# A Fourier transform feeding a gated layer: VectorE's PSUM reads in a row, GpSimd's sums and folds behind a wait, two buffers for folded chunks

## The chip, the cores and the metric

The kernel runs on one core of one Trainium2 chip. The metric is the device time of one execution in microseconds (us). A core has five engines with instruction queues of their own: TensorE (PE in the profile; PEld is its weight load), VectorE (DVE), ScalarE (ACT), GpSimd (POOL) and SyncE (SP, which here only issues DMAs). They wait for each other by semaphores. SBUF is the on-chip memory, PSUM the accumulators that TensorE writes.

## The reference, cut to what matters

```python
x                       # 8 x 3008 x 256, float32
X = fft(fft(x, axis=1), axis=2).real      # rows become 24064 tokens of 256
h = X @ w_in            # w_in 256 x 2048
g = h * cos(h)
out = g @ w_out         # w_out 2048 x 256
```

## The kernel before, in words

The Fourier transform over the 256 columns is folded into the weights `w_in` once, at the start. The transform over the 3008 rows is done for each of 8 batches in two halves by matmuls with constant matrices. *First half*: the batch is loaded (`load_x`, in two parts) and cut into 8 chunks. `fold` (L240) adds and subtracts mirrored columns of a chunk into the buffer `xf`, on GpSimd for all batches but the first, with a small column copy on ScalarE (L247). `first_half` multiplies it (pz, L282 and L285), ScalarE copies the result (zs), and `store_z` sends it to DRAM. *Second half*: `load_z` brings it back, `second_half` (pb, L327) makes six groups of it, `pq`, with a row `nb` for each group that goes out and back by DMA. A group holds 256 tokens (225 in group 0, whose steps are the "short" ones), and each is worked on together with its mirror image in the batch: side sg = 0 and side sg = 1.

The layer then runs in *steps*. A step is one group and one of 8 pairs of blocks of the 2048 hidden columns, so there are 8 steps in a group, 48 in a batch, 384 in all. The main loop (L741) writes out by hand the order in which step t of each part is issued, as a software pipeline: `cur` is step t, `prev` t-1, `old` t-2, `done` t-3. For one step s the parts are:

- `seed` (ScalarE, L453): puts the norm's part of h into a PSUM bank H, one step ahead. Three banks H rotate.
- mm1 (TensorE, L483), first half with WC, then second half with WS, both added into H. Between them `act_e` (ScalarE, L494) copies the first half's result times two into `ew`.
- h (VectorE, L499, `dve_h`): `ew` minus H, the mirror side. It reads H in PSUM.
- two roundings (ScalarE, L514) of H and of h into r.
- frac0 and frac1 (VectorE, L518, `dve_frac`): r minus H and r minus h. The first reads H in PSUM, the second reads only SBUF.
- the sin (ScalarE, L524) over both sides, after frac1.
- g0 and g1 (VectorE, L528, `dve_g`): (H - 0.25) r and (h - 0.25) r. The first reads PSUM, the second only SBUF.
- s0, s1, s2 (VectorE, L539, L546, L548, `dve_s` with k = 0, 1, 2): sums of r into S, which let seven products stand for eight. All read only SBUF.
- mm2 (TensorE, L572): seven matmuls m0 to m6, in the trace two instructions each, four before mm1's second half of a later step and three behind it. m6, alone in the group M<-S,w, is the one that reads what s2 wrote.

VectorE's order in one pass of the loop is g0(old), g1(old), frac0(prev), s0(old), frac1(prev), s1(old), h(cur), s2(old). TensorE's is mm1(cur) first half, m0 to m3 of done, mm1(cur) second half, m4 to m6 of done.

When a group's 8 steps are through, ScalarE takes the seven sums out of PSUM (mr, L593), GpSimd adds them up with six instructions (L611 to L621, into `cb`), and `store_out` transposes `cb` on VectorE (L664), once for each side, and issues the output DMAs on SyncE. The six sums are issued in a row; only their inputs hold them up. The transposes come two and three steps after `take_m`'s first part. For the last group `combine_last` does all this on VectorE, TensorE and ScalarE.

The next batch's transform is spread over the steps of the current one by `transform`, a table from a step's number in the batch to calls: x loaded at steps 3 and 14, chunk folds at 6, 9, 14, 17 and so on (both halves of a fold in the same step), their first halves 2 or 4 steps later, z stored one step after that, z loaded at 39, and the six second halves at 42 to 47.

Of the kernel before, what the change touches and what calls it, by code (L numbers as in the profile page):

```python
# [121 lines left out]
def kernel(  # L122
# [102 lines left out]
    nc.gpsimd.memset(xf[0:XR, 512:1024:128], 0.0)  # L225

    bank = {"fft": 1, "M": 4, "H": 3}

# [2 lines left out]


    def folded(b, c):
        return xf if b else xf0[c % 2]

    def fold(b, c, e):
        lo = IP * (c % 4)
        xv = xs[c // 4].rearrange("r (i d) -> r i d", d=ND)[0:XR, lo : lo + IP]
        fv = folded(b, c).rearrange("r (e i d) -> r e i d", e=2, d=128)[0:XR]
        (nc.gpsimd if b else nc.vector).tensor_tensor(  # L240
            out=fv[:, e, :, 1:128],
            in0=xv[:, :, 1:128],
            in1=xv[:, :, 255:128:-1],
            op=ALU.subtract if e else ALU.add,
        )
        if e == 0:
            (nc.scalar.copy if b else nc.gpsimd.tensor_copy)(  # L247
                out=fv[:, 0, :, 0], in_=xv[:, :, 0]
            )

    def middle(b, p):
        xm = xs[p].rearrange("r (i d) -> r i d", d=ND)[0:XR, :, 128]
# [67 lines left out]
    def second_half(b, g):  # L320

        T = _width(g)
        z2 = z2s[b]
        pb = psum("pb")
        for q in range(4):
            jj = 4 * g + q
            nc.tensor.matmul(  # L327
                pb[:, 128 * q : 128 * q + 128],
                lhsT=z2[:, jj * 128 : jj * 128 + 128],
                rhs=BJ[:, jj * 128 : jj * 128 + 128],  # L330
                start=True,
                stop=True,
            )
# [12 lines left out]
        if b == 0 and g == 0:  # L346
            return
        nd = dpool.tile([1, 256], FP, tag="nd", bufs=4, name="nd")
        nc.sync.dma_start(out=nd[:, 0:T], in_=pq[0:1, T : 2 * T])
        nc.sync.dma_start(out=nb[:, 0:T], in_=nd[0:1, 0:T].to_broadcast([128, T]))  # L350


    def spread_norm():
# [3 lines left out]
        nc.tensor.matmul(pn[:, 0:T], lhsT=ones, rhs=pq[0:1, T : 2 * T], start=True, stop=True)  # L357
        nc.scalar.copy(out=nb[:, 0:T], in_=pn[:, 0:T])

    def transform(b):  # L360
        todo = {}

        def at(o, *call):
            todo.setdefault(o, []).append(call)
# [167 lines left out]
    def dve_s(s, k):  # L532
        T = s.T
        gv = s.r[:, 0 : 4 * T].rearrange("p (q t) -> p q t", q=4)
        if k == 0:
            s.S = spool.tile([128, 1024], FP, tag="S", bufs=2, name="S")
        sv = s.S[:, 0 : 4 * T].rearrange("p (q t) -> p q t", q=4)
        if k == 0:
            nc.vector.tensor_tensor(  # L539
                out=sv[:, 0:2],  # L540
                in0=gv[:, 2:3].to_broadcast([128, 2, T]),
                in1=gv[:, 0:4:3],
                op=ALU.subtract,
            )
        elif k == 1:
            nc.vector.tensor_tensor(out=sv[:, 2], in0=sv[:, 1], in1=gv[:, 0], op=ALU.subtract)  # L546
        else:
            nc.vector.tensor_tensor(out=sv[:, 3], in0=gv[:, 1], in1=sv[:, 2], op=ALU.add)  # L548

    def mm2(s, part):  # L550
        T = s.T
# [47 lines left out]
    def combine_m(s):  # L599
        T = s.T  # L600
        key = (s.b, s.grp)
        acc.pop(key)
        mv = mrs.pop(key).rearrange("p (m t) -> p m t", m=7)[:, :, 0:T]
        cb = spool.tile([128, 7 * 256], FP, tag="cb", bufs=1, name="cb")
        cf = cb.rearrange("p (m t) -> p m t", m=7)
        cv = [cf[:, m, 256 - T : 256] if m in (2, 3) else cf[:, m, 0:T] for m in range(7)]
        if T < 256:
            nc.gpsimd.memset(cf[:, 0:2, T:256], 0.0)
            nc.gpsimd.memset(cf[:, 2:4, 0 : 256 - T], 0.0)
        tt = nc.gpsimd.tensor_tensor  # L610
        tt(out=cv[0], in0=mv[:, 0], in1=mv[:, 1], op=ALU.add)  # L611
        tt(out=cv[4], in0=mv[:, 0], in1=mv[:, 5], op=ALU.subtract)
        tt(
            out=cf[:, 5:7, 0:T],
            in0=cf[:, 4:5, 0:T].to_broadcast([128, 2, T]),
            in1=mv[:, 3:5],
            op=ALU.add,
        )
        tt(out=cv[1], in0=cv[6], in1=mv[:, 6], op=ALU.add)
        tt(out=cv[2], in0=cv[5], in1=mv[:, 2], op=ALU.add)  # L620
        tt(out=cv[3], in0=cv[5], in1=mv[:, 4], op=ALU.add)  # L621
        outs[key] = cb

    def combine_last(s):
        key = (s.b, s.grp)
# [111 lines left out]
    def step(t, last=None):  # L737
        s = steps[t] if 0 <= t < n else None
        return s if s is not None and (last is None or s.fp == 7) else None

    for t in range(n + LAG + 1):  # L741
        cur, prev, old, done = step(t), step(t - 1), step(t - 2), step(t - LAG)
        if cur:
            if t % per == 0:
                todo = transform(cur.b + 1) if cur.b + 1 < NB else {}
            mm1(cur, 0)
            act_e(cur)
            if t == 0:
# [44 lines left out]
        for call in todo.pop(t % per, ()):  # L793
            call[0](*call[1:])


# [28 lines left out]
```

## Time and profile before

| | |
|---|---|
| median of 3 runs | 1974.6 us (1972.9 to 1975.87) |
| the profiled execution's own time | 1975.47 us |
| its span, first to last instruction | 1973.7 us |
| mean granted TensorE clock | 0.994 |
| busy: TensorE, VectorE, ScalarE, GpSimd | 1946.2, 1858.0, 1504.2, 467.7 us |

The span is taken in the execution that was profiled, so terms from the trace are set against that execution's own time. In rows of groups the columns are line, engine, operation, output<-input and count, then busy time in us, mean ns of one instruction, then the idle time of the engine just ahead of them and what ended it. In rows of the timeline they are the start in us, the duration in us, the engine, line, operation, output<-input and count; in brackets the idle time before and what released it. TensorE's ends are modelled, so its pace is better read from starts.

### The profile page before, as it was taken

To read this page: it belongs to the slowest core of one execution; us is meant where nothing else is said; L and a number is where in the kernel's file an instruction comes from. 1 tells how busy PE (TensorE), PEld (TensorE's weight loads), DVE (VectorE), ACT (ScalarE), POOL (GpSimd) and SP (SyncE) were. 2 spreads that over 40 slices of the span, in tenths; PEclk is the share of its full clock that TensorE was granted. 3 is DMA by queue.
4 is the path that set the end of the run, shared out by engine and by line. 5 is a ranking of instruction groups with operands and counts; after the bars stand their busy time and mean duration, and the time that the engine had idled before them with its cause. 6 is when DMAs were issued, how large, how long until landed. Compare 5 with 4: busy or idle time off the path is not lost.

```text
span 1973.7 us, 28641 instructions
## 1 busy us (share of the span) xinstructions
PE 1946.2 (99%) x9216; PEld 1686.8 (85%) x9216; DVE 1858.0 (94%) x3217; ACT 1504.2 (76%) x2762; POOL 467.7 (24%) x431
## 2 busy tenths in 40 slices
PE   7999999999999999999999999999999999999998
PEld 3888899888988889888898888988889888898887
DVE  4999989999899998999989999999999999899998
ACT  2877777777777778777877777777877787778775
POOL 2133113231133212323122222123311233112111
PEclk7999999999999999999999999999999999999999
DMA  6321121211202012020121101221022200210000
GB/s 196 94 59 29 47 59 27 53 31 51 59 16 59 24 51 58 21 59 23 49 57 28 52 23 53 60 53 25 20 57 59 54 19 21 62 22 10 19 15 22
DMA packets 159957, 88.65 MB, mean 45 GB/s; under 512 B 104845, under 2 KB 150204, under 8 KB 158656
## 3 DMA queue, kind: packets, MB, share of 16 engines
q1 hardware_dynamic: 158320, 85.72, 16.7%
q8 instruction: 74, 1.21, 0.3%
q10 hardware_dynamic: 1392, 1.05, 0.2%
q14 instruction: 75, 0.61, 0.1%
q0 software_dynamic: 96, 0.05, 0.0%
HBM read 49.51 MB, written 37.28 MB: 44 GB/s over the span
## 4 chain that ended last, share of the span: by engine, by line
PE 91%; DVE 5%; DMA 2%; ACT 1%; issue 1%; SPq 0%; ACTq 0%; POOL 0%; DVEq 0%; POOLq 0%
PE M L572 54%; PE H L483 32%; PE pz L285 3%; PE pb L327 2%; DVE r L528 1%; DMA out_dram<-ob 1%; DVE S L548 1%; DVE S L546 1%; DMA xp<-in_x_dram 1%; DVE r L518 0%; DVE S L539 0%; DMA zd<-zs 0%; DVE h L499 0%; DVE ob L664 0%; SPq L674 0%
## 5 line engine op out<-in xcount | busy, mean ns | idle before, releaser
L524 ACT ACTIVATE r<-r 128x1024 f32<-128x1024 f32 (+1 forms) x384 | 398.5, 1038 | 284.3 <-DVE r L518 283.4
L572 PE MATMUL M<-S,VX 128*128 128x256 f32 (+1 forms) x2304 | 612.7, 375 | 0.0
L572 PEld LDWEIGHTS M<-S,VX 128*128 128x128 f32 x2304 | 438.3, 190 | 49.4
L483 PE MATMUL H<-pq,WS 128*128 128x256 f32 (+1 forms) x1536 | 390.8, 377 | 7.8 <-ACT ew L494 7.5
L483 PE MATMUL H<-pq,WC 128*128 128x256 f32 (+1 forms) x1536 | 395.1, 380 | 1.1 <-ACT H L453 1.1
L572 PE MATMUL M<-r,w 128*128 128x256 f32 (+1 forms) x1536 | 387.9, 375 | 0.0
L453 ACT ACTIVATE H<-nb,wn 128x256 f32<-128x256 f32 (+1 forms) x766 | 363.5, 475 | 17.1 <-DVE r L528 3.2
L483 PEld LDWEIGHTS H<-pq,WC 128*128 128x128 f32 x1536 | 284.1, 191 | 73.6 <-ACT r L514 29.2
L499 DVE TENSOR_TENSOR h<-ew,H 128x512 f32<-128x512 f32 (+1 forms) x384 | 257.1, 670 | 87.3 <-PE H L483 81.0
L483 PEld LDWEIGHTS H<-pq,WS 128*128 128x128 f32 x1536 | 290.9, 191 | 49.9 <-ACT ew L494 15.9
L572 PEld LDWEIGHTS M<-r,w 128*128 128x128 f32 x1536 | 300.5, 196 | 27.0
L518 DVE SCALAR_TENSOR_TENSOR r<-r,h 128x512 f32<-128x512 f32 (+1 forms) x384 | 309.7, 806 | 0.0
L240 POOL TENSOR_TENSOR xf<-xp 110x508 f32<-110x508 f32 x112 | 164.9, 1493 | 585.4 <-PE pz L285 540.9
L539 DVE TENSOR_TENSOR S<-r 128x512 f32<-128x512 f32 (+1 forms) x384 | 286.8, 747 | 0.1
L528 DVE SCALAR_TENSOR_TENSOR r<-h,r 128x512 f32<-128x512 f32 (+1 forms) x384 | 272.3, 709 | 0.0
L514 ACT ACTIVATE r<-H 128x512 f32<-128x512 f32 (+1 forms) x384 | 223.0, 581 | 57.1 <-DVE h L499 54.1
L494 ACT ACTIVATE ew<-H 128x512 f32<-128x512 f32 (+1 forms) x384 | 225.7, 588 | 45.5 <-PE H L483 40.3
L518 DVE SCALAR_TENSOR_TENSOR r<-r,H 128x512 f32<-128x512 f32 (+1 forms) x384 | 255.4, 665 | 0.0
L528 DVE SCALAR_TENSOR_TENSOR r<-H,r 128x512 f32<-128x512 f32 (+1 forms) x384 | 254.4, 662 | 0.8 <-ACT r L524 0.8
L514 ACT ACTIVATE r<-h 128x512 f32<-128x512 f32 (+1 forms) x384 | 236.2, 615 | 0.0
L572 PE MATMUL M<-S,w 128*128 128x256 f32 (+1 forms) x768 | 225.4, 375 | 0.0
L572 PE MATMUL M<-r,VX 128*128 128x256 f32 (+1 forms) x768 | 225.2, 375 | 0.0
(79 smaller groups left out, 1497.9 us busy)
## 6 DMA issues: line engine op xcount, KB each, us to landing
out_dram<-ob SPq DMA_DIRECT2D x728, 32.0 KB
xp<-in_x_dram SPq DMA_DIRECT2D x48, 256.0 KB
zd<-zs SPq DMA_DIRECT2D x128, 80.0 KB
z<-zd SPq DMA_DIRECT2D x8, 1280.0 KB
xp<-in_x_dram SPq DMA_DIRECT2D x38, 240.0 KB
nb<-nd SPq DMA_DIRECT2D x40, 128.0 KB
wr<-in_moe_w_in_dram SPq DMA_DIRECT2D x4, 512.0 KB
w<-in_moe_w_out_dram SPq DMA_DIRECT2D x2, 1024.0 KB
```

The costliest lines, as they stand in the source:

```text
L240: (nc.gpsimd if b else nc.vector).tensor_tensor(out=fv[:, e, :, 1:128], in0=xv[:, :, 1:128], in1=xv[:, :, 255:128:-1], op=ALU.subtract if ...
L285: nc.tensor.matmul(pz[rows, a:512], lhsT=w, rhs=fv[:, e, a:512], start=True, stop=True)
L453: nc.scalar.activation(out=s.H[:, u * T : u * T + T], in_=s.nb[:, 0:T], func=AF.Copy, bias=0.25, scale=wn[:, f : f + 1],)
L483: nc.tensor.matmul(s.H[:, u * T : u * T + T], lhsT=W[:, 128 * f : 128 * f + 128], rhs=s.pq[:, e * T : e * T + T], start=False, stop=True, ...
L494: nc.scalar.mul(out=s.ew[:, 0 : 2 * s.T], in_=s.H[:, 0 : 2 * s.T], mul=2.0)
L499: nc.vector.tensor_tensor(out=s.h[:, 0 : 2 * T].rearrange("p (u t) -> p u t", u=2)[:, :, ::-1], in0=s.ew[:, 0 : 2 * T].rearrange("p (u t) ...
L514: nc.scalar.activation(out=r, in_=h, func=AF.Copy, bias=BIG, scale=1.0)
L518: nc.vector.scalar_tensor_tensor(out=r, in0=r, scalar=-BIG, in1=h, op0=ALU.add, op1=ALU.subtract)
L524: nc.scalar.activation(out=r, in_=r, func=AF.Sin, bias=0.0, scale=SIN_SCALE)
L528: nc.vector.scalar_tensor_tensor(out=r, in0=h, scalar=-0.25, in1=r, op0=ALU.add, op1=ALU.mult)
L539: nc.vector.tensor_tensor(out=sv[:, 0:2], in0=gv[:, 2:3].to_broadcast([128, 2, T]), in1=gv[:, 0:4:3], op=ALU.subtract,)
L572: nc.tensor.matmul(acc[key][m // 2][:, 256 * (m % 2) : 256 * (m % 2) + T], lhsT=w, rhs=a, start=first, stop=s.fp == 7, skip_group_check=True,)
```

## The change

There are five edits.

1. VectorE's order in one pass becomes g0(old), frac0(prev), g1(old), frac1(prev), s0(old), s2(done), s1(old), h(cur). Seen from h, the three instructions that read PSUM follow each other: h, then g0 and frac0 of the next pass. s2 is made one pass later than before, in the pass in which m6 reads it.
2. GpSimd's sums and folds are no longer issued where they arise. They are put into a table `aside` by step; in each pass they are issued after h with an added dependency on that pass's s1, the instruction ahead of h. A group's sums come at its following group's steps 3 (two), 4, 5 and 6 (two); a chunk's fold in two successive steps.
3. There are two folded-chunk buffers for the later batches instead of one.
4. `transform` spaces the work anew: folds at 7, 9, 15, 17 and so on with the second half a step later, first halves two steps after a fold's start, z stored a step after that, z loaded at 37, second halves at 41, 43, 45, 49, 52 and 55, so that the last three lie in the next batch's first steps.
5. The transposes and output stores come two steps later; `nb` has 6 buffers instead of 8; the small column copy is issued ahead of the fold instead of behind it.

The diff's core:

```diff
-    xf = cpool.tile([128, 2 * IP * 128], FP, tag="xf", name="xf")
+    xf1 = [cpool.tile([128, 2 * IP * 128], FP, tag=f"xf{i}", name="xf") for i in range(2)]
...
-        return xf if b else xf0[c % 2]
+        return (xf1 if b else xf0)[c % 2]
...
-        nb = spool.tile([128, 256], FP, tag="nb", bufs=8, name="nb")
+        nb = spool.tile([128, 256], FP, tag="nb", bufs=6, name="nb")
...
-        for q in range(4):
-            for c, o, f in ((2 * q, 6, 8), (2 * q + 1, 9, 13)):
-                at(8 * q + o, fold, b, c, 0)
-                at(8 * q + o, fold, b, c, 1)
-                at(8 * q + f, first_half, b, c)
-                at(8 * q + f + 1, store_z, b, c, 0)
-                at(8 * q + f + 1, store_z, b, c, 1)
-        at(39, load_z, b, 0)
-        at(39, load_z, b, 1)
-        for g in range(NG):
-            at(42 + g, second_half, b, g)
-        return todo
+        for c in range(NCH):
+            o = 7 + 8 * (c // 2) + 2 * (c % 2)
+            aside.setdefault(t0 + o, []).append((fold, b, c, 0))
+            aside.setdefault(t0 + o + 1, []).append((fold, b, c, 1))
+            at(o + 2, first_half, b, c)
+            at(o + 3, store_z, b, c, 0)
+            at(o + 3, store_z, b, c, 1)
+        at(37, load_z, b, 0)
+        at(37, load_z, b, 1)
+        for g, o in enumerate((41, 43, 45, 49, 52, 55)):
+            at(o, second_half, b, g)
...
+        t0 = NG * 8 * s.b + 8 * s.grp + 7 + LAG + 1
+        for k, group in enumerate(sums):
+            for o, a, b in group:
+                aside.setdefault(t0 + k, []).append((add, o, a, b, o is cv[4]))
...
+    def beside(ins, ahead):
+        if ahead is not None:
+            tc.add_manual_dep(
+                ins.ins,
+                ahead.ins.name,
+                mybir.DependencyInfo(mybir.DependencyClass.Sync, mybir.DependencyReason.DATA),
+                reason="start with the PSUM reads",
+            )
...
         if old:
             dve_g(old, 0)
-            dve_g(old, 1)
         if step(t + 1):
             seed(step(t + 1))
         if prev:
             dve_frac(prev, 0)
         if old:
-            dve_s(old, 0)
+            dve_g(old, 1)
         if prev:
             dve_frac(prev, 1)
             act_sin(prev)
         if old:
-            dve_s(old, 1)
+            dve_s(old, 0)
+        if done:
+            dve_s(done, 2)
+        ahead = dve_s(old, 1) if old else None
...
-        if old:
-            dve_s(old, 2)
-        if step(t - LAG - 2, True):
-            store_out(step(t - LAG - 2), 0)
-        if step(t - LAG - 3, True):
-            store_out(step(t - LAG - 3), 1)
+        for call in aside.pop(t, ()):
+            beside(call[0](*call[1:]), ahead)
+        if step(t - LAG - 4, True):
+            store_out(step(t - LAG - 4), 0)
+        if step(t - LAG - 5, True):
+            store_out(step(t - LAG - 5), 1)
```

More of the change, by code (lines that the diff above doesn't have):

```diff
@@ L223 @@
     nrow = cpool.tile([1, NDFF], FP, tag="nrow", name="nrow")
-    xf = cpool.tile([128, 2 * IP * 128], FP, tag="xf", name="xf")
-    nc.gpsimd.memset(xf[0:XR, 512:1024:128], 0.0)
+    xf1 = [cpool.tile([128, 2 * IP * 128], FP, tag=f"xf{i}", name="xf") for i in range(2)]
+    for xf in xf1:
+        nc.gpsimd.memset(xf[0:XR, 512:1024:128], 0.0)
     bank = {"fft": 1, "M": 4, "H": 3}
@@ L239, in fold @@
         fv = folded(b, c).rearrange("r (e i d) -> r e i d", e=2, d=128)[0:XR]
-        (nc.gpsimd if b else nc.vector).tensor_tensor(
+        if e == 0:
+            (nc.scalar.copy if b else nc.gpsimd.tensor_copy)(
+                out=fv[:, 0, :, 0], in_=xv[:, :, 0]
+            )
+        return (nc.gpsimd if b else nc.vector).tensor_tensor(
             out=fv[:, e, :, 1:128],
@@ L245, in fold @@
         )
[L246 to L249, printed above, removed]
     def middle(b, p):
@@ L538, in dve_s @@
         if k == 0:
-            nc.vector.tensor_tensor(
+            return nc.vector.tensor_tensor(
                 out=sv[:, 0:2],
@@ L544, in dve_s @@
             )
-        elif k == 1:
-            nc.vector.tensor_tensor(out=sv[:, 2], in0=sv[:, 1], in1=gv[:, 0], op=ALU.subtract)
-        else:
-            nc.vector.tensor_tensor(out=sv[:, 3], in0=gv[:, 1], in1=sv[:, 2], op=ALU.add)
+        if k == 1:
+            o, a, b, op = 2, sv[:, 1], gv[:, 0], ALU.subtract
+        else:
+            o, a, b, op = 3, gv[:, 1], sv[:, 2], ALU.add
+        return nc.vector.tensor_tensor(out=sv[:, o], in0=a, in1=b, op=op)
     def mm2(s, part):
@@ L609, in combine_m, with add @@
             nc.gpsimd.memset(cf[:, 2:4, 0 : 256 - T], 0.0)
[L610 to L617, printed above, removed]
-        )
[L619 to L622, printed above, removed]
+        wide = (cf[:, 5:7, 0:T], cf[:, 4:5, 0:T].to_broadcast([128, 2, T]), mv[:, 3:5])
+        sums = (
+            ((cv[0], mv[:, 0], mv[:, 1]), (cv[4], mv[:, 0], mv[:, 5])),
+            (wide,),
+            ((cv[1], cv[6], mv[:, 6]),),
+            ((cv[2], cv[5], mv[:, 2]), (cv[3], cv[5], mv[:, 4])),
+        )
+        t0 = NG * 8 * s.b + 8 * s.grp + 7 + LAG + 1
+        for k, group in enumerate(sums):
+            for o, a, b in group:
+                aside.setdefault(t0 + k, []).append((add, o, a, b, o is cv[4]))
+    def add(o, a, b, less):
+        return nc.gpsimd.tensor_tensor(
+            out=o, in0=a, in1=b, op=ALU.subtract if less else ALU.add
+        )
     def combine_last(s):
@@ L743 @@
         if cur:
-            if t % per == 0:
-                todo = transform(cur.b + 1) if cur.b + 1 < NB else {}
+            if t % per == 0 and cur.b + 1 < NB:
+                transform(cur.b + 1)
             mm1(cur, 0)
@@ L784 @@
             act_round(cur, 1)
-        if old:
-            dve_s(old, 2)
-        if step(t - LAG - 2, True):
-            store_out(step(t - LAG - 2), 0)
-        if step(t - LAG - 3, True):
-            store_out(step(t - LAG - 3), 1)
+        for call in aside.pop(t, ()):
[4 more added lines that the diff above has]
+            store_out(step(t - LAG - 5), 1)
         for call in opening.pop(t, ()):
             call[0](*call[1:])
-        for call in todo.pop(t % per, ()):
+        for call in todo.pop(t, ()):
             call[0](*call[1:])
```

8 lines of the change are left out of this document (6 added, 2 removed).

## The prediction

> **What bounds the kernel now.** I read the page first, then the boundaries between batches as windows, then the durations of VectorE's instructions, then the timeline. Names of steps and operations are those of the section on the kernel.
>
> ```profile
> span 1973.7 us, 28641 instructions
> PE 1946.2 (99%) x9216; PEld 1686.8 (85%) x9216; DVE 1858.0 (94%) x3217; ACT 1504.2 (76%) x2762; POOL 467.7 (24%) x431
> PE 91%; DVE 5%; DMA 2%; ACT 1%; issue 1%; SPq 0%; ACTq 0%; POOL 0%; DVEq 0%; POOLq 0%
> L483 PE MATMUL H<-pq,WS 128*128 128x256 f32 (+1 forms) x1536 | 390.8, 377 | 7.8 <-ACT ew L494 7.5
> ```
>
> TensorE is busy 99% of the span and is 91% of the chain that ended last. So a faster VectorE, at 94%, is worth only what TensorE still waits for. The fourth row names such a wait: the second half of mm1 (WS) waits for ew. To place it, windows of 26 us over the seven boundaries between batches, 240.8 us apart; after the bounds and the length come the busy time and count of PE, PEld, DVE, ACT and POOL:
>
> ```profile
> 300.40:326.40 26.00, 24.79 (x127) 23.46 (x126) 25.89 (x47) 19.67 (x40) 9.17 (x8) 1.00 0.09 21
> ...
> 1504.40:1530.40 26.00, 24.79 (x126) 23.47 (x125) 25.94 (x47) 19.66 (x40) 9.18 (x8) 1.00 0.09 21
> 1745.20:1771.20 26.00, 26.00 (x135) 25.18 (x134) 25.94 (x51) 20.43 (x41) 6.41 (x8) 1.00 0.09 21
> ```
>
> Six windows look like the first two rows: TensorE is idle for 1.21 us, and some nine matmuls are missing. The seventh loses nothing. It is the one after which no batch is left to be folded, and its GpSimd time is 6.41 instead of 9.17 us. The stall therefore goes with the folds. One boundary in order of time (start, us, engine):
>
> ```profile
> 790.62 3.02 POOL L240 TENSOR_TENSOR xf<-xp 110x508 f32<-110x508 f32 x2
> 791.07 1.46 DVE L546 TENSOR_TENSOR S<-S,r 128x225 f32<-128x225 f32 x1
> 791.49 0.92 PE L483 MATMUL H<-pq,WC 128*128 128x225 f32 x4
> 792.25 0.93 PE L572 MATMUL M<-r,w 128*128 128x225 f32 x4
> 792.45 0.61 DVE L499 TENSOR_TENSOR h<-ew,H 128x450 f32<-128x450 f32 x1
> 793.09 0.55 ACT L514 ACTIVATE r<-H 128x450 f32<-128x450 f32 x1 [0.96 <-DVE h L499]
> 793.39 0.54 PE L572 MATMUL M<-S,VX 128*128 128x225 f32 x2
> 794.00 0.54 ACT L494 ACTIVATE ew<-H 128x450 f32<-128x450 f32 x1
> 794.59 1.03 PE L483 MATMUL H<-pq,WS 128*128 128x225 f32 x4 [0.65 <-ACT ew L494]
> ...
> 798.50 0.54 PE L572 MATMUL M<-S,VX 128*128 128x225 f32 x2
> 799.54 1.03 PE L483 MATMUL H<-pq,WS 128*128 128x225 f32 x4 [0.50 <-ACT ew L494]
> ...
> 803.46 0.54 PE L572 MATMUL M<-S,VX 128*128 128x225 f32 x2
> 804.05 1.03 PE L483 MATMUL H<-pq,WS 128*128 128x225 f32 x4
> ```
>
> Two folds hold GpSimd for 3 us, s1 beside them takes 1.46 us, h starts late, the rounding waits for h, ew comes behind the rounding, and mm1 waits for ew. Its size: four short matmuls are 0.76 us apart (791.49 to 792.25), so 0.19 each. The pair at 793.39 was due to be followed at 793.77 and was followed at 794.59: 0.82 us lost. In the same way 0.66 and 0.21 are lost at 799.54 and 804.05. After each of the three stalls the four matmuls take 1.03 instead of 0.92: about 0.1 more each. Together **2.0 us for one boundary**, 12.0 for six.
>
> Why s1 takes 1.46 (min/median/max in ns):
>
> ```profile
> L499 DVE TENSOR_TENSOR h<-ew,H x384: 604/675/690, 48.9 to 1955.7; 128x512 f32<-128x512 f32 x160, 128x450 f32<-128x450 f32 x32
> L518 DVE SCALAR_TENSOR_TENSOR r<-r,H x384: 601/675/687, 53.2 to 1957.8; 128x512 f32<-128x512 f32 x160, 128x450 f32<-128x450 f32 x32
> L518 DVE SCALAR_TENSOR_TENSOR r<-r,h x384: 608/679/1750, 53.7 to 1959.0; 128x512 f32<-128x512 f32 x160, 128x450 f32<-128x450 f32 x32
> L664 DVE STREAM_TRANSPOSE ob<-cb x94: 695/703/717, 105.1 to 1947.5; 128x512 f32<-128x512 f32 x94
> L240 POOL TENSOR_TENSOR xf<-xp x112: 1259/1640/1801, 72.0 to 1656.1; 110x508 f32<-110x508 f32 x112
> ```
>
> The instructions that read H, in PSUM, and the transpose, with one input, never go over 717 ns. The same instruction on h, two inputs in SBUF, goes from 608 to 1750. GpSimd's fold goes from 1259 to 1801.
>
> **The change, part by part.** First the step as it is, when nothing disturbs it:
>
> ```profile
> 1926.87 0.69 DVE L499 TENSOR_TENSOR h<-ew,H 128x512 f32<-128x512 f32 x1 [0.39 <-PE H L483]
> 1927.47 0.42 DVE L548 TENSOR_TENSOR S<-r,S 128x256 f32<-128x256 f32 x1
> 1927.59 0.60 ACT L514 ACTIVATE r<-H 128x512 f32<-128x512 f32 x1 [0.36 <-DVE h L499]
> 1927.81 0.68 DVE L528 SCALAR_TENSOR_TENSOR r<-H,r 128x512 f32<-128x512 f32 x1
> ...
> 1930.48 1.03 PE L483 MATMUL H<-pq,WS 128*128 128x256 f32 x4
> 1930.81 0.41 DVE L546 TENSOR_TENSOR S<-S,r 128x256 f32<-128x256 f32 x1
> ...
> 1931.34 1.03 PE L572 MATMUL M<-S,VX 128*128 128x256 f32 x4
> 1931.62 0.69 DVE L499 TENSOR_TENSOR h<-ew,H 128x512 f32<-128x512 f32 x1 [0.39 <-PE H L483]
> 1932.21 0.60 PE L572 MATMUL M<-S,w 128*128 128x256 f32 x2
> ```
>
> From h to h is 4.75 us. VectorE's wide instructions follow each other by 0.60 (h to s2), its narrow ones by 0.34, and it idles 0.39 before h. TensorE's matmuls are 0.216 apart (1930.48 to 1931.34, four).
>
> *GpSimd's waits.* Each sum or fold now starts when s1 is done, so beside h, g0 and frac0, which all read H; g1, the next with two SBUF inputs, starts about 2.0 us after h. Behind the waiting GpSimd instruction stands only the next sum or fold, a step later. Two narrow sums or one fold are the most that one step gets. A fold alone is 1.26 us, and it fits. For the case that it doesn't, here is a collision:
>
> ```profile
> 908.63 1.23 POOL L621 TENSOR_TENSOR cb<-cb,mr 128x256 f32<-128x256 f32 x1
> ...
> 909.20 1.21 DVE L518 SCALAR_TENSOR_TENSOR r<-r,h 128x512 f32<-128x512 f32 x1
> ```
>
> frac1 was stretched by 0.53, and 0.68 before its end is 909.73, near the end of the sum at 909.86: it looks as if it stood still until GpSimd was done. The Trainium skill, SBUF — State Buffer, section "Who interferes with whom", says that whichever of two such instructions starts first keeps the shared ports to its end. By that rule the trace agrees, and an overrun costs only its own length; taken as a fixed price it would be 0.53 a step. My sum holds neither.
>
> So VectorE loses its collisions, the three stalls of a boundary have no cause left, and the gain is 6 x 2.0 = **-12.0 us**. All else that VectorE saves is hidden behind TensorE. What is late next is s2, below. The pb products spread over steps 41 to 55 put three of them, work that TensorE has to do anyway, into the short steps of the boundary, which gives VectorE more room there; no gain is put down for it.
>
> *The new order.* h, g0, frac0, g1, frac1, s0, s2 of the step before, s1. Two things follow. First, frac0 is now third after h and needs the first rounding, which waits for h: it starts at 0.72 after h, ends at 1.32, so frac0 starts at 1.37 instead of 1.20. VectorE loses 0.17 a step; its need becomes 4.43 of 4.75, hidden. Second, s2 used to be ready a step ahead of its reader, the last matmul m6 (M<-S,w); now it is made in the same step. After h: g1 at 1.97, frac1 2.57, s0 3.17, s2 from 3.77 to 4.19. m6 starts at 5.34 (1932.21). Less about 0.25 for its weight load and the signal, **0.9 us are to spare**. A transpose between h and g0 puts 0.62 in and takes out the 0.17: 0.45 later, 0.45 to spare; the second one a step later starts 0.13 behind, 0.32 to spare. In the short steps I estimate instructions 0.07 shorter (0.61 for h at 792.45), and the same walk leaves 0.2 to 0.3 at the tightest. So no stall: 0, bounded by 0 and by 0.3 in each of 2 x 47 transpose steps. The sin, behind frac1, starts 0.6 earlier; nobody gains by it.
>
> *The tail.* After the last step TensorE has no mm1, so m6 comes after 12 matmuls instead of 20, and the last two transposes, moved two steps later, fall just ahead of it:
>
> ```profile
> 1943.38 9.84 SPq L674 DMA_DIRECT2D out_dram<-ob  x16
> ...
> 1954.22 1.03 PE L483 MATMUL H<-pq,WS 128*128 128x256 f32 x4
> 1956.38 1.03 PE L572 MATMUL M<-r,w 128*128 128x256 f32 x4
> ```
>
> m6 would be due at 1956.38 + 12 x 0.216 = 1958.97. h can start 1.14 after WS (1930.48 to 1931.62), at 1955.36, plus 0.13 of lag; s2 ends 4.64 later, at 1960.13. With signal and refill **+1.3 us**, bounded by 0 and 1.5. The 16 output DMAs of these transposes, 9.84 us on SyncE's queue, move two steps (9.5 us) later and end near 1962.7, ahead of the last stores, which come after m6: 0.
>
> *The opening.* Before the pipeline is full the same s2 stands on the path once: between 0 and one instruction (0.60); I take **+0.2**, since its early steps have fill-in work ahead of m6.
>
> *At nothing:* the second folded buffer (a fold now comes two steps ahead of its pz, 9 us for 1.26 us of work), six nb buffers (the last reader of each lies 9 steps or more before the next writing), x loaded four steps instead of three before its first fold, z loaded four instead of three before pb. If one of these covers failed, pz or pb would show a wait. SyncE's queue gets no DMA more: the z stores shift by one or two steps, the output stores by two, and x and z have the step more that was just named to land behind them.
>
> **Sum:** -12.0 + 1.3 + 0.2 = -10.5 us. The profiled execution took 1975.47 (its span 1973.7 and 1.8 around it) and lies 0.9 over the median of the three runs, 1974.6. From 1975.47 that gives 1965.0; from the median **1964.1 us**.
>
> **The rivals.**
>
> *s2 holds up m6 (slower).* The point is the 0.32 to spare after the second transpose. For it: the walk is by hand, a few terms of 0.05 to 0.1 each, and the rounding can be late behind mr copies. Against it: the order still has 0.3 of slack a step. If m6 came 0.3 late in each of the 2 x 47 transpose steps: 28 us, so 1964.1 + 28 = 1992.
>
> *The collisions stay (no change).* If a sum or fold starts late, or reaches past frac0, g1 and frac1 stretch as they do now, and the boundary stalls as now. For it: folds of 1801 ns exist, those that collided. Against it: 2.0 us of room. It gives 1974.6 + 1.5 = 1976, or half the gain where only the folds collide: 1970.
>
> *The tail and opening cost nothing:* 1974.6 - 12.0 = 1962.6. This is part of the forecast's spread.
>
> **How the numbers follow.** Forecast, 1961.5 to 1967: 0.71. Half the gain, 1967 to 1974: 0.09, of which 0.05 still under 1970.6. No change or slightly slower, 1974 to 1978.5: 0.06. m6, over 1978.5: 0.14. The bound of 0.2%, about what a measurement of this kernel can tell from no change, is 3.9 us. Faster 0.76, same 0.10, slower 0.14. The range goes from 1961.5 (1962.6 less about 1 for the scatter that 1975.47 against 1974.6 shows) to 1974, which leaves out the last two cases.
>
> **What would show it.** Right: L518 on h, L528 on h, L539 and L546 with maxima near their medians; VectorE's busy time well down; the boundary windows at 26.0 us of PE like the seventh; frac0 starting about 1.37 after h. Wrong: an idle time of PE before M<-S,w that is released by S L548 anywhere but in the tail and opening (the first rival), or GpSimd's instructions beside L518 on h (the second).

## The result and the profile after

| | before | changed |
|---|---|---|
| median | 1974.31 us (6 runs, 1972.9 to 1975.87) | 1964.28 us (6 runs, 1963.37 to 1965.47) |
| ratio | | 0.9949, 95% interval 0.9936 to 0.9962 |
| the profiled execution: own time, span | 1975.47, 1973.7 us | 1964.43, 1962.7 us |

The changed kernel is 10.0 us faster; 10.5 were forecast, 1964.1 us in all. The forecast's mechanism can be followed line by line. In the page of the changed kernel:

```profile
span 1962.7 us, 29008 instructions
PE 1940.6 (99%) x9216; PEld 1689.6 (86%) x9216; DVE 1747.2 (89%) x3217; ACT 1521.2 (78%) x2762; POOL 377.7 (19%) x432
PE 97%; DMA 1%; DVE 1%; ACT 0%; issue 0%; ACTq 0%; POOL 0%; DVEq 0%; POOLq 0%; SPq 0%
L484 PE MATMUL H<-pq,WS 128*128 128x256 f32 (+1 forms) x1536 | 388.8, 376 | 0.6 <-ACT ew L495 0.5
L574 PE MATMUL M<-S,w 128*128 128x256 f32 (+1 forms) x768 | 225.7, 375 | 1.0 <-DVE S L550 1.0
```

VectorE's count of instructions is the same, but it is busy for 111 us less and GpSimd for 90 us less: nearly all of it is time in which they stood in each other's way. VectorE's share of the chain that ended last went from 5% to 1%. TensorE's wait for ew went from 7.5 to 0.6 us. In its place stands a single wait of 1.0 us of m6 for s2 (S L550 is s1 and s2 here). The boundary windows (columns as before the change) have no idle TensorE left. They do not hold the same steps as before, since the kernel is some 2 us further ahead at each boundary and half of pb now lies there, so only TensorE's busy time compares:

```profile
300.40:326.40 26.00, 26.00 (x144) 25.77 (x143) 23.78 (x49) 20.63 (x40) 6.86 (x8) 1.00 0.26 74
...
1504.40:1530.40 26.00, 26.00 (x143) 24.52 (x142) 22.65 (x46) 20.64 (x41) 7.37 (x9) 1.00 0.18 39
1745.20:1771.20 26.00, 26.00 (x137) 25.07 (x136) 24.90 (x48) 21.17 (x40) 1.65 (x4) 1.00 0.12 29
```

TensorE's starts give the size. From the first matmul of one batch's first step (H<-pq,WC) to that of the next it takes 240.8 us before and 238.8 us in the changed kernel, in each of the six batches from the second to the seventh: 2.01 us less a batch.

The durations of the same instructions, min/median/max in ns:

```profile
L519 DVE SCALAR_TENSOR_TENSOR r<-r,H x384: 601/687/693, 52.9 to 1945.0; 128x512 f32<-128x512 f32 x160, 128x450 f32<-128x450 f32 x32
L519 DVE SCALAR_TENSOR_TENSOR r<-r,h x384: 609/684/698, 53.5 to 1946.2; 128x512 f32<-128x512 f32 x160, 128x450 f32<-128x450 f32 x32
L245 POOL TENSOR_TENSOR xf<-xp x112: 1253/1265/1280, 79.3 to 1650.0; 110x508 f32<-110x508 f32 x112
```

The frac on h had a maximum of 1750 and has 698. The fold went from 1259 to 1801 and now takes 1.28 us at most. The other instructions that read only SBUF end the same way: the maxima of g1, s0, s1 and s2 are 694, 699, 433 and 432. So no collision is left on either side. One step in order of time, with two sums in it:

```profile
1923.40 0.42 DVE L550 TENSOR_TENSOR S<-S,r 128x256 f32<-128x256 f32 x1
...
1923.96 1.42 POOL L626 TENSOR_TENSOR cb<-mr 128x256 f32<-128x256 f32 x2 [22.39 <-DVE S L550]
1924.05 0.69 DVE L500 TENSOR_TENSOR h<-ew,H 128x512 f32<-128x512 f32 x1 [0.23 <-PE H L484]
1924.65 0.69 DVE L529 SCALAR_TENSOR_TENSOR r<-H,r 128x512 f32<-128x512 f32 x1
1924.77 0.60 ACT L515 ACTIVATE r<-H 128x512 f32<-128x512 f32 x1 [0.17 <-DVE h L500]
1925.40 0.69 DVE L519 SCALAR_TENSOR_TENSOR r<-r,H 128x512 f32<-128x512 f32 x1
1926.00 0.69 DVE L529 SCALAR_TENSOR_TENSOR r<-h,r 128x512 f32<-128x512 f32 x1
```

s1 ends at 1923.82, the sums start 0.14 later and end at 1925.38, and g1, the next instruction with two SBUF inputs, starts at 1926.00. frac0 starts 1.35 after h (1.37 in the walk), because it waits for the rounding.

### The profile page after: what moved, and what is told of

Same layout as the page of the kernel before. It is cut to its first block, busy times and chain, and to the rows that moved or that the text cites. A ratio compares the mean times of both kernels' runs of the same rounds, so it can differ in the third digit from the quotient of the medians.

```text
span 1962.7 us, 29008 instructions
## 1 busy us (share of the span) xinstructions
PE 1940.6 (99%) x9216; PEld 1689.6 (86%) x9216; DVE 1747.2 (89%) x3217; ACT 1521.2 (78%) x2762; POOL 377.7 (19%) x432
## 4 chain that ended last, share of the span: by engine, by line
PE 97%; DMA 1%; DVE 1%; ACT 0%; issue 0%; ACTq 0%; POOL 0%; DVEq 0%; POOLq 0%; SPq 0%
PE M L574 58%; PE H L484 34%; PE pz L286 3%; PE pb L328 2%; DMA xp<-in_x_dram 1%; DMA zd<-zs 0%; PE pw L388 0%; DMA z<-zd 0%; PE M L256 0%; DVE r L519 0%; PE pz L283 0%; PE H L470 0%; DVE xp L206 0%; POOL xf L242 0%; DVE ob L670 0%
## 5 line engine op out<-in xcount | busy, mean ns | idle before, releaser
L626 POOL TENSOR_TENSOR cb<-cb,mr 128x256 f32<-128x256 f32 (+3 forms) x188 | 157.9, 850 | 541.4 <-DVE S L550 344.5
L540 DVE TENSOR_TENSOR S<-r 128x512 f32<-128x512 f32 (+1 forms) x384 | 259.1, 675 | 0.1
L519 DVE SCALAR_TENSOR_TENSOR r<-r,h 128x512 f32<-128x512 f32 (+1 forms) x384 | 258.6, 673 | 0.0
L529 DVE SCALAR_TENSOR_TENSOR r<-h,r 128x512 f32<-128x512 f32 (+1 forms) x384 | 258.2, 672 | 0.0
L245 POOL TENSOR_TENSOR xf<-xp 110x508 f32<-110x508 f32 x112 | 141.7, 1265 | 436.1 <-DVE S L550 281.6
```

What stands on the lines that cost most here:

```text
L245: return (nc.gpsimd if b else nc.vector).tensor_tensor(out=fv[:, e, :, 1:128], in0=xv[:, :, 1:128], in1=xv[:, :, 255:128:-1], op=ALU.subtr ...
L519: nc.vector.scalar_tensor_tensor(out=r, in0=r, scalar=-BIG, in1=h, op0=ALU.add, op1=ALU.subtract)
L529: nc.vector.scalar_tensor_tensor(out=r, in0=h, scalar=-0.25, in1=r, op0=ALU.add, op1=ALU.mult)
L540: return nc.vector.tensor_tensor(out=sv[:, 0:2], in0=gv[:, 2:3].to_broadcast([128, 2, T]), in1=gv[:, 0:4:3], op=ALU.subtract,)
L626: return nc.gpsimd.tensor_tensor(out=o, in0=a, in1=b, op=ALU.subtract if less else ALU.add)
```

## The experiments

The forecast came out, but a time that agrees does not show which of the five edits made it. Theory A is the prediction's: the gain is that GpSimd no longer stands beside VectorE's two-input SBUF instructions, and waits and order make it together. Theory B is that the new spacing makes it: pb in the boundary's short steps, folds out of it. Theory C is that pacing alone makes it, one or two GpSimd pieces a step, wherever they stand. Theory D came up on the way and concerns the second buffer. Each ratio is to the kernel before, run on the same chip. No run takes back the later transposes and stores, the six `nb` buffers or the place of the column copy by itself, and none has the new order alone, with the old spacing and one buffer.

| run | median us | ratio, 95% interval |
|---|---|---|
| waits taken out | 2068.37 | 1.048, 1.0466 to 1.0494 |
| waits kept, VectorE's old order | 1972.28 | 0.9991, 0.9982 to 0.9999 |
| new spacing and buffers alone | 2019.93 | 1.0233, 1.0219 to 1.0246 |
| pb back at steps 42 to 47 | 1963.02 | 0.9945, 0.9933 to 0.9957 |
| start beside g1 instead of h | 2090.09 | 1.059, 1.0574 to 1.0606 |
| s2 of the same step behind s1 | 1963.48 | 0.9954, 0.9942 to 0.9967 |
| kernel before, two buffers alone | 2006.13 | 1.0167, 1.0154 to 1.0181 |
| s2 one instruction later | 1973.14 | 0.9992, 0.9983 to 1.0001 |
| tail: s2 early in the last passes | 1962.25 | 0.9945, 0.9933 to 0.9958 |
| one buffer, odd chunks a step later | 1964.26 | 0.9943, 0.9929 to 0.9957 |

**The waits taken out.**

```diff
         for call in aside.pop(t, ()):
-            beside(call[0](*call[1:]), ahead)
+            call[0](*call[1:])
```

> The changed kernel with one thing taken out: the added dependency of GpSimd's sums and folds on s1. VectorE's order, the two buffers and the new spacing stay. Theory A (the gain comes from keeping GpSimd off VectorE's two-input SBUF instructions, and this is the waits' work): with nothing to hold them, the sums run in a row again and folds start as soon as x is there, L519 and L529 on h and L540 get maxima over 1.1 us again, the boundary stalls come back (at least 2.0 us each), and since s2 now has less than 1 us to spare, m6 may be held up in other groups too: 1974 or more. Theory B (the gain comes from the new spacing: pb products in the short steps, folds out of the boundary): 1964.3, within 1 us.

2068.37 us: 104 slower than the changed kernel. Theory B falls, and theory A had the direction but, with "1974 or more", not the size. GpSimd does its pieces as soon as their inputs are there. In the timeline of this kernel, GpSimd first:

```profile
901.29 3.59 POOL L626 TENSOR_TENSOR cb<-cb,mr 128x512 f32<-128x512 f32 x4
904.85 6.48 POOL L245 TENSOR_TENSOR xf<-xp 110x508 f32<-110x508 f32 x4
```

VectorE in the same stretch:

```profile
905.38 1.75 DVE L519 SCALAR_TENSOR_TENSOR r<-r,h 128x512 f32<-128x512 f32 x1
907.05 1.75 DVE L540 TENSOR_TENSOR S<-r 128x512 f32<-128x512 f32 x1
908.72 1.48 DVE L550 TENSOR_TENSOR S<-r,S 128x256 f32<-128x256 f32 x1
910.12 1.48 DVE L550 TENSOR_TENSOR S<-S,r 128x256 f32<-128x256 f32 x1
```

And TensorE. It waited for the third of these, s2 (S<-r,S), which ended at 910.20:

```profile
910.25 0.71 PE L574 MATMUL M<-S,w 128*128 128x256 f32 x2 [2.08 <-DVE S L550]
910.80 1.66 PE L484 MATMUL H<-pq,WC 128*128 128x256 f32 x4
912.25 1.91 PE L574 MATMUL M<-r,w 128*128 128x256 f32 x4
```

Four sums and four folds stand in a row of ten us. Each of VectorE's four two-input instructions is 1.07 us longer than its median, s2 comes two us late, and m6 waits 2.08 us. And then the matmuls are slow: four take 1.66 and 1.91 us instead of 1.03. The mean granted clock of three stretches of two us is in the column behind POOL:

```profile
908.00:910.00 2.00, 0.17 (x1) 0.00 (x0) 2.00 (x2) 0.22 (x1) 2.00 (x3) 1.00 0.00 0
910.00:912.00 2.00, 1.75 (x6) 1.50 (x7) 2.00 (x3) 0.00 (x0) 1.32 (x1) 0.76 0.00 0
912.00:914.00 2.00, 2.00 (x7) 1.55 (x6) 1.94 (x4) 1.77 (x4) 0.00 (x0) 0.50 0.00 0
```

The clock goes to 0.50 at 911.0 and stays there for 3.41 us. The ten matmuls from 910.80 to 914.64 would take 2.16 us at 0.216 and take 3.84, so 1.7 us more. So this stall is paid for almost twice, and 15 stalls of this run are followed by such a stretch: by the same 1.7 us each an estimated 26 of the 104 us. The waits are what makes this order and this spacing bearable at all.

**The waits kept, VectorE's old order.** The pass is again g0, g1, frac0, s0, frac1, s1, h, s2 of the same step:

```diff
         if old:
             dve_g(old, 0)
+            dve_g(old, 1)
...
-            dve_g(old, 1)
+            dve_s(old, 0)
...
-        if old:
-            dve_s(old, 0)
-        if done:
-            dve_s(done, 2)
         ahead = dve_s(old, 1) if old else None
...
             act_round(cur, 1)
+        if old:
+            dve_s(old, 2)
```

> The changed kernel with VectorE's old order (g0, g1, frac0, s0, frac1, s1, h, s2 of the same step); waits on s1, buffers and spacing stay. Theory A in its strict form (the PSUM reads must stand in a row): the window is only h, s2 collides with every fold and sum by up to 0.5 us and g1 with the second sum; it is hidden in the long steps, and in the boundary up to half of the stall comes back: 1963 to 1969, of which the tail gives 1.3 back. Theory B (spacing): 1963.0, that is 1964.3 less the tail's 1.3, with the collisions there but hidden.

1972.28 us, a gain of 2 instead of 10; more was lost than either theory expected. s2 stands between h and g0 and is the instruction that GpSimd meets:

```profile
L550 DVE TENSOR_TENSOR S<-S,r x384: 375/411/432, 55.6 to 1959.2; 128x256 f32<-128x256 f32 x160, 128x225 f32<-128x225 f32 x32
L550 DVE TENSOR_TENSOR S<-r,S x384: 375/635/1419, 56.4 to 1959.7; 128x256 f32<-128x256 f32 x160, 128x225 f32<-128x225 f32 x32
```

The second row is s2, with a median of 635 ns; the first, s1, is never touched. TensorE's loads for the second half of mm1 waited 46 times for ew, and 44 of these waits lie in steps 10 to 35 of a batch, long steps in which GpSimd has folds and sums to do. The row of the waits (engine and tile, what it waited for, us in all, times, the longest):

```profile
PEld H L484 <- ACT ew L495: 16.6, 46, 1.4
```

In the changed kernel there are 3 such waits; in the kernel before there were 23, of 15.9 us in all. By the starts of mm1 the short steps of a boundary take as long here as in the changed kernel, but a batch takes 240.4 us instead of 238.8, and all of that is lost in the long steps. So with the new spacing the waits are enough to clear the boundary, and without the order the loss moves to the long steps. The waits without the order are worth about a fifth of the gain, by the interval between almost nothing and a third.

**The spacing and the buffers alone, on the kernel before.** In `transform` folds, first halves, z and pb take their new steps; two folded buffers, six of nb; no `aside`, no waits, old order.

```diff
-            for c, o, f in ((2 * q, 6, 8), (2 * q + 1, 9, 13)):
+        for c in range(NCH):
+            o = 7 + 8 * (c // 2) + 2 * (c % 2)
+            at(o, fold, b, c, 0)
+            at(o + 1, fold, b, c, 1)
...
-        return xf if b else xf0[c % 2]
+        return (xf1 if b else xf0)[c % 2]
```

> The kernel before with the new spacing alone: two folded buffers, folds, first halves, z and pb at their new steps; sums in a row, VectorE's old order, no waits. Theory A: the sums still collide in the boundary's short steps, so most of the stall stays: 1969 to 1974. Theory B: the whole gain without the tail's price, 1962.5 to 1964.

2019.93 us: neither theory saw that this makes the kernel 46 us slower. GpSimd's timeline in this kernel says why:

```profile
883.25 1.09 POOL L612 TENSOR_TENSOR cb<-mr 128x256 f32<-128x256 f32 x1 [2.17 <-ACT mr L593]
...
887.80 1.24 POOL L621 TENSOR_TENSOR cb<-cb,mr 128x256 f32<-128x256 f32 x1
889.00 6.26 POOL L241 TENSOR_TENSOR xf<-xp 110x508 f32<-110x508 f32 x4
```

From 883.25 to 895.26 GpSimd hardly rests: five sums and four folds. In the kernel before the folds stand apart:

```profile
908.63 1.23 POOL L621 TENSOR_TENSOR cb<-cb,mr 128x256 f32<-128x256 f32 x1
917.08 2.94 POOL L240 TENSOR_TENSOR xf<-xp 110x508 f32<-110x508 f32 x2 [7.22 <-PE pz L285]
```

There a fold was released by pz, for with one buffer it had to wait until the chunk before was read. This is theory D: the single buffer was GpSimd's pacing. The step at which the program issues an instruction sets its place in its engine's queue and not its time: here GpSimd ran ahead of the steps in which the folds were issued, since nothing but their inputs held them.

**Two buffers alone, on the kernel before.**

```diff
-    xf = cpool.tile([128, 2 * IP * 128], FP, tag="xf", name="xf")
+    xf1 = [cpool.tile([128, 2 * IP * 128], FP, tag=f"xf{i}", name="xf") for i in range(2)]
...
-        return xf if b else xf0[c % 2]
+        return (xf1 if b else xf0)[c % 2]
```

> The kernel before with the two folded-chunk buffers (and six nb buffers) alone; steps, order and sums as before. Theory D, formed from the trace of the spacing alone (there GpSimd runs six sums and four folds in one row of 13 us): the single buffer was GpSimd's pacing, since a fold had to wait for the pz that read the chunk before, and the second buffer takes it away: 2000 to 2030. Rival (the new steps are what costs 46 us there): 1974 within 2.

2006.13 us: theory D holds. A buffer that lets work start earlier costs 32 us here, the new steps on top of it another 14. The six `nb` buffers are in this run too; no wait for a transfer into `nb` shows in its trace. In the timeline of this kernel the folds follow the sums without a gap:

```profile
881.97 1.23 POOL L622 TENSOR_TENSOR cb<-cb,mr 128x256 f32<-128x256 f32 x1
883.16 3.12 POOL L241 TENSOR_TENSOR xf<-xp 110x508 f32<-110x508 f32 x2
```

**One buffer in the changed kernel.** Two runs. In the first only the buffer was taken away:

> The changed kernel with one folded-chunk buffer instead of two, waits, order and spacing as changed. The fold of an odd chunk must now also wait for the pz of the chunk before, which comes at the end of the very step in which the fold is to start, so that it starts with the next step's g1 and frac1. Theory A: 28 such folds collide as in the run with the start beside g1, but each of these steps has a pz more on TensorE (1.0 us); between nothing and 0.5 us each, 1964 to 1978. Rival (the second buffer is no part of the gain once the waits are there): 1964.3 within 1.

It took 1987.33 us, but this is no answer: as the next expectation says, a fold there overwrites what pz was still to read, so this kernel computes something else. The second:

```diff
-    xf1 = [cpool.tile([128, 2 * IP * 128], FP, tag=f"xf{i}", name="xf") for i in range(2)]
+    xf1 = [cpool.tile([128, 2 * IP * 128], FP, tag=f"xf{i}", name="xf") for i in range(1)]
...
-        return (xf1 if b else xf0)[c % 2]
+        return xf1[0] if b else xf0[c % 2]
...
-            o = 7 + 8 * (c // 2) + 2 * (c % 2)
+            o = 7 + 8 * (c // 2) + 3 * (c % 2)
```

> The changed kernel with one folded-chunk buffer and the odd chunks' folds, first halves and z stores one step later, so that each fold still comes in a step after the pz that read the buffer before, and can start at s1. In the run with one buffer before this one, the fold of an odd chunk stood ahead of that pz in the program and overwrote what it was to read: that kernel computed something else, and its 1987 us answer no question of the study. Theory A (the waits are the pacing, the second buffer only makes room for it): no collision, no stall, 1964.3 within 1. Rival (a second buffer is worth something by itself): over 1967.

1964.26 us, the changed kernel's time. With the waits there, the second buffer is worth nothing by itself: it is room for a spacing of two steps between chunks, and three steps do as well. But "no collision" did not come out. A fold and two sums now fall into one step in places; they take 1.26 and 1.42 us, more than the 2.0 us of the window, and 26 times g1 or frac1 is stretched. The row of g1:

```profile
L529 DVE SCALAR_TENSOR_TENSOR r<-h,r x384: 602/684/1216, 55.9 to 1948.3; 128x512 f32<-128x512 f32 x160, 128x450 f32<-128x450 f32 x32
```

All 26 lie in steps that hold a pz, which take 5.85 us instead of 4.75, and a batch still takes 238.8 us. So a collision does not have to cost time: these met steps that had room for them.

**pb back at its old steps.**

```diff
-        for g, o in enumerate((41, 43, 45, 49, 52, 55)):
+        for g, o in enumerate((42, 43, 44, 45, 46, 47)):
```

> The changed kernel with the six second halves (pb) back at steps 42 to 47, so that no pb stands in the boundary's short steps; all else changed. Theory A: there is no collision to pay for, so no stall, 1964.3 within 0.7; by the walk the tightest short steps have 0.2 to 0.3 us to spare for s2, so at most 0.3 a boundary. Theory B (pb fills what VectorE cannot follow): the short steps stall again, 1968 to 1976.

1963.02 us, and its first boundary window has TensorE busy for 26.00 us as well. Its interval and the changed kernel's overlap, so nothing tells the two apart. The new places of pb, which the prediction had at no gain, give none.

**The start beside g1.** GpSimd waits for frac0 instead of s1; the pieces and steps are the same.

```diff
-            dve_frac(prev, 0)
+        ahead = dve_frac(prev, 0) if prev else None
...
-        ahead = dve_s(old, 1) if old else None
+        if old:
+            dve_s(old, 1)
```

> The changed kernel with the added dependency on frac0 in place of s1: GpSimd gets the same pieces in the same steps, but each starts when frac0 is done, beside g1, frac1 and s0, which read only SBUF. Theory A (what counts is where in the step a piece stands: beside the PSUM reads): every piece meets two-input SBUF instructions, VectorE needs 4.4 plus 0.6 to 1.2 us in the steps with a piece, over TensorE's 4.75, and m6 waits: some 300 steps at 0.2 to 0.75 us less what pz and pb give back, so 2010 to 2150. Theory C (pacing alone: one or two pieces a step instead of a run of ten, wherever they stand): 1964 to 1972.

2090.09 us, inside theory A's range, and theory C falls: the same pacing at another place in the step is 126 us slower than the changed kernel. The frac on h, beside which the pieces now run:

```profile
L519 DVE SCALAR_TENSOR_TENSOR r<-r,h x384: 607/1218/1764, 53.3 to 2072.1; 128x512 f32<-128x512 f32 x160, 128x450 f32<-128x450 f32 x32
```

And m6's waits for s2:

```profile
PEld M L574 <- DVE S L550: 132.8, 174, 2.0
```

The median of the frac is 1218 ns instead of 684, so it collides in most steps, and m6 waits 174 times.

**s2 one instruction later.** This measures the price that the prediction gave to the slower rival.

```diff
+        ahead = dve_s(old, 1) if old else None
         if done:
-            dve_s(done, 2)
-        ahead = dve_s(old, 1) if old else None
+            ahead = dve_s(done, 2)
```

> The changed kernel with s1 and s2 exchanged (s0, s1, s2 of the step before, h; GpSimd waits for that s2). s2 comes 0.34 us later for the narrow instruction ahead of it, and about 0.12 more because s1 now follows s0 directly: 0.46. This takes from the room of s2 ahead of m6 and from nothing else. In the changed kernel's trace the end of s2 lies 0.54 us on average before the start of m6 in the step behind the second transpose (0.17 at the least in mid-run), 0.75 in the one before it, about 1.1 else; some 0.25 of it is needed for weights and signal. Theory A (the price of the new order is this room, and it decides at zero): a wait of m6 for s2 of 0.1 to 0.3 in each group, some 50 to 70 in all, 1970 to 1976, hence most of the gain gone. Rival (the room is larger than the starts show): 1964.3 within 1.

1973.14 us, as expected: 0.46 us later, without a single collision, and nearly all of the gain is gone. The room that the changed kernel has is seen at one of the tight places, behind a second transpose (changed kernel, VectorE and TensorE):

```profile
523.75 0.71 DVE L670 STREAM_TRANSPOSE ob<-cb 128x512 f32<-128x512 f32 x1
...
527.35 0.42 DVE L550 TENSOR_TENSOR S<-r,S 128x256 f32<-128x256 f32 x1
...
528.17 0.59 PE L574 MATMUL M<-S,w 128*128 128x256 f32 x2
```

s2 ends at 527.77, m6 starts at 528.17: 0.40. With s2 0.46 later, m6 waits. m6's waits in the kernel with s2 later:

```profile
PEld M L574 <- DVE S L550: 16.2, 48, 2.0
```

And in the changed kernel:

```profile
PEld M L574 <- DVE S L550: 1.6, 2, 1.4
```

**s2 of the same step, behind s1.** The PSUM reads still stand in a row, and m6 gets its step of room back.

```diff
-        if done:
-            dve_s(done, 2)
-        ahead = dve_s(old, 1) if old else None
+        if old:
+            dve_s(old, 1)
+        ahead = dve_s(old, 2) if old else None
```

> The changed kernel with s2 of the same step directly behind s1 and ahead of h (s0, s1, s2, h), GpSimd waiting for that s2. The PSUM reads still stand in a row, and m6 has its step to spare again. Theory A: no collisions; the tail's and the opening's price of s2 is gone, 1963.0, unless the two waits of s1 and s2 for the instruction just ahead of them (estimated at 0.14 us each, since each starts only when the other is done) use up the 0.3 us a step that VectorE has left: then up to 1968. Rival (that s2 was moved to the pass of its reader is itself part of the gain): over 1970.

1963.48 us: that s2 moved to the pass of its reader is no part of the gain. The estimate of 0.14 for each wait was nearly right; s1 follows s0 by 0.72 instead of 0.60, and s2 follows s1 by 0.46 instead of 0.34:

```profile
902.17 0.68 DVE L540 TENSOR_TENSOR S<-r 128x512 f32<-128x512 f32 x1
902.89 0.43 DVE L550 TENSOR_TENSOR S<-S,r 128x256 f32<-128x256 f32 x1
903.35 0.42 DVE L550 TENSOR_TENSOR S<-r,S 128x256 f32<-128x256 f32 x1
```

**The tail.**

```diff
-        if done:
+        if done and t < n:
             dve_s(done, 2)
...
+        if old and t >= n - 1:
+            dve_s(old, 2)
```

> The changed kernel; only in the last passes s2 is made one pass earlier, as in the kernel before (from the last pass with an h on). Theory A: the wait of m6 for s2 at 1947.83 in the changed kernel, 1.2 us by its starts, goes, and nothing else changes: 1963.1, ratio to the changed kernel 0.9994. Rival (the end is set by the output stores or by the last transposes): 1964.3.

In the changed kernel TensorE's last m6 but two (a pair of matmuls) starts late:

```profile
1945.36 1.46 PE L574 MATMUL M<-S,VX 128*128 128x256 f32 x6
1947.83 0.71 PE L574 MATMUL M<-S,w 128*128 128x256 f32 x2 [1.01 <-DVE S L550]
```

Here it does not, and comes 1.29 after the start of its neighbours, six matmuls at 0.216:

```profile
1943.82 1.46 PE L574 MATMUL M<-S,VX 128*128 128x256 f32 x6
1945.11 0.59 PE L574 MATMUL M<-S,w 128*128 128x256 f32 x2
```

The median is 1962.25 us, the lowest of all versions here, but its interval overlaps the changed kernel's. That the stall is gone is shown by the trace; that the time is lower is not shown by the runs. It beats the kernel before, and by its trace it is the changed kernel without its one wait for s2 in the tail.

## Why the prediction was right, point by point

- *The boundary, -12.0.* It held: no idle time is left in any window, the six batches are 2.01 us shorter each by TensorE's starts, 12.1 in all, and the cause was the one named. What each part of the change does for it was not worked out. The runs show it: the waits in the old order give 2 us, for they clear the boundary and most of that is lost again in the long steps; the order and spacing without the waits cost 94.
- *The fold fits into the 2.0 us beside the PSUM reads.* It held: fold 1.27 us at most 1.28, two sums 1.42, and g1 1.95 after h (1924.05 to 1926.00).
- *frac0 waits for the rounding, 0.17 a step, hidden.* 0.15, hidden.
- *The room of s2, 0.9, 0.45 and 0.32 after 0.25 for weights and signal.* The second transpose's step was to leave 0.57 to m6's start; its steps show 0.54 on average where they hold no pz or pb, 0.61 in the median of all, 0.40 in the row above and 0.17 at the least before the tail. No row was shown for the 0.25. In the two places where m6 waits, it starts 0.05 and 0.06 after s2's end and takes 0.11 longer, so by these two it needs some 0.17. That it costs nothing held; that it decides was shown by the exchange.
- *The tail, +1.3.* The pair of matmuls at 1947.83 was due 1.29 after 1945.36, at 1946.65: 1.18 late, and it takes 0.71 instead of 0.60. So 1.29 were lost.
- *The opening, +0.2.* In the changed kernel m6 waits for s2 once there (the other of the two waits above); the row is at 62.03 us, and the pair takes 0.66 instead of 0.55, some 0.15 in all with its late start; by the starts of mm1 the opening loses 0.27, of which 0.1 lies ahead of the second half of mm1 just before:

```profile
62.03 0.66 PE L574 MATMUL M<-S,w 128*128 128x225 f32 x2
```

- *The sum.* By the traces -12.1, 1.3 and 0.3 make -10.5. Two small gains were not foreseen: the first step starts 0.2 earlier, and the seventh boundary, which had no stall, is 0.3 shorter. Together this is the 11.0 us between the two spans. The medians differ by 10.0; the rest lies within the scatter of the runs, some 3 us before and 2 us after.
- *At nothing: buffers, nb, x and z a step earlier, pb.* As a whole they cost nothing. But the second buffer's entry, "a fold now comes two steps ahead of its pz", overlooked what the single buffer did: it paced GpSimd. Only because the waits pace it now is the second buffer free.
- *The rival "the collisions stay", priced at 1970 to 1976.* It did not happen. Its price holds for the old order with the waits, where s2 collides: 1972.28. In the new order it was wrong by far: where the waits are missing or the place is wrong the time is 2068 and 2090. The price took today's boundary stall, in which VectorE may be late by more than a us because s2 is a step ahead. In the new order a collision of 1.07 meets 0.4 to 0.9 us of room, in every group and not in the boundary alone, and a long stall can also cost the clock.
- *The rival "s2 holds up m6".* It did not happen. Forced by making s2 0.46 us later, it cost 9 us (1964.28 to 1973.14) with 48 waits. The price of 28 us, 0.3 in each of 94 steps, was not reached.

## What to carry to other kernels

Two engines whose instructions stretch each other are kept apart by *where in the step* one starts, and a handle for it is a wait on the instruction after which the other runs for a while only what is not stretched: here the wait in the old order gave 2 us, the new order and spacing without it cost 94, and both together gave 10. A collision costs only what the step has no room for, so look at the steps without spare time first. A buffer that makes a producer wait can be its pacing; before adding a second one, look at what releases the producer, and put another wait in its place. When work is moved closer to its reader, count the room that is left in every kind of step, for that room sets the price of every later disturbance.

## What the runs showed of the hardware that was not expected

The granted clock can drop after a stall of TensorE that is not long, and the length alone does not decide. In the kernel with the spacing alone TensorE waits for ew once in each batch from the second to the seventh, six times for 2.15 us by its starts. Three of these stalls are followed by a granted clock of 0.50 for 3.41 us, and three by the full clock. One of each kind, the stall ending at 358.98 and at 605.55:

```profile
355.00:359.00 4.00, 2.01 (x11) 1.45 (x9) 4.00 (x7) 2.73 (x5) 1.41 (x1) 1.00 0.00 0
359.00:361.00 2.00, 2.00 (x9) 1.80 (x10) 2.00 (x4) 0.81 (x2) 0.00 (x0) 1.00 0.20 44
...
603.00:606.60 3.60, 1.60 (x8) 1.10 (x7) 3.60 (x8) 2.49 (x5) 0.00 (x0) 1.00 0.04 9
606.60:610.00 3.40, 3.40 (x10) 2.69 (x9) 3.40 (x7) 2.06 (x3) 0.00 (x0) 0.50 0.25 56
```

What differs is where the stall lies. In each of these traces all changes of the granted clock stand at multiples of 3.413 us from one another, as on a grid, and every low stretch in mid-run lasts one interval of it. The kernels without waits and with the spacing alone have 30 stalls of about 1.5 us or more behind the opening, of which 18 are followed by the low clock. Each of the 18 has at least 2.15 us of idle TensorE within one interval of the grid. Of the other 12, which mostly lie across two intervals, eleven have at most 1.93 in any one, and one has 2.16. So the limit in these runs lies near 2.15 of 3.41 us; the longest stall without a drop is 2.53 us, split into 1.83 and 0.70.

The Trainium skill, TensorE: Matmul & The Clock Gate, section "Why this matters for your kernels", asks for no idle gaps of TensorE above about 3 us if the clock is to stay up. Here 2.15 us within one interval was enough, so the measurement is the stricter of the two.

VectorE's wide instructions are a little longer in the median in the changed kernel, although it has no collisions: those that read PSUM by 6 to 12 ns (frac0 from 675 to 687), those that read only SBUF by 5 to 8 (frac1 from 679 to 684). Why is open.
